# Loads of r, k and v from tile 9 on: issued by ScalarE instead of SyncE

## The chip, the cores and the metric

The kernel runs on one core of a Trainium2 chip. The core has five engines that run beside each other, each with its own in-order stream of instructions: TensorE (PE in the profile, its weight loads PEld), VectorE (DVE), ScalarE (ACT), GpSimd (POOL) and SyncE (SP). Transfers are done by 16 DMA engines; an instruction on SP or on ACT starts one. The metric is the time of one execution in microseconds of device time, smaller is better. The median of three runs before the change is 156.64 us (156.24 to 156.75).

## The reference

Two stages follow each other. The first is a linear attention with a decaying state, for batch 4, 8 heads, 768 time steps and head width 48:

```
for t in range(S):
    cur   = einsum('bhd,bhe->bhde', u * k[t], v[t])
    y[t]  = einsum('bhd,bhde->bhe', r[t], state + cur)
    state = w * state + einsum('bhd,bhe->bhde', k[t], v[t])
```

Its output, with the heads side by side, is x of shape (4, 768, 384). The second stage is a feed-forward block with a normalisation ahead of it and a residual:

```
xn  = (x - mean(x)) / sqrt(var(x) + 1e-6) * g_ln
out = x + relu(xn @ w_ch1) @ w_ch2        # 384 -> 1536 -> 384
```

All inputs and the output are 32-bit floats in the chip's main memory (HBM).

## The kernel before, in words

The 768 steps are cut into 6 chunks of 128, and a chunk of one batch entry is a tile: 24 tiles, numbered so that the four batch entries of a chunk follow each other. Every tile goes through the same steps. Each step is a small Python function with a two- or three-letter name, called with a tile's (or a block's) number and a letter for the engine: `v` is DVE, `s` is ACT, `g` is POOL, and `-` is a step whose engine is fixed.

For tile i the steps are these. LR, LK and LV load r, k and v (192 KB each, in runs of 48 floats; lines 326, 323 and 329). SR and SK multiply r and k by powers of the decay (line 194), CV turns v to bf16 (189 on ACT, 191 on POOL or DVE). TKR transposes both scaled tensors by DMA (line 490; tiles from 8 on; the earlier tiles are transposed on PE). AT multiplies them into the attention matrix (364), AM masks it, Q and S make the term with u and the state, CC copies a small result, VB and X put x together (427, 452). SQ and XN do the statistics and the centring (459; 465 on ACT, 467 elsewhere), LT2 (two tiles at once, line 484) or LTD (one tile, 480) transposes the centred tile by DMA. UP multiplies by the first weight (520) and RL is its relu (536 on ACT, 538 on DVE), DN multiplies by the second weight (548), OT adds the residual (604) and STO stores the tile (611, on SP or on ACT by its letter).

The feed-forward block works on groups of one or two tiles. UP writes into two PSUM buffers in turn, so the UP after the next one needs the RL of this one to be done. The loaded r, k and v have rings of 11 buffers each, the transposed tiles of 3, the centred tiles of 4.

The order of all this is one list, PLAN, written out in the source. A loop at the end of the kernel calls the steps in that order. Each engine carries out its own steps in the order of the list; waits between engines are added from the data and the buffers. So a step that is late holds up the steps that stand behind it in the list on the same engine, also when they need nothing of it. Every DMA also takes one of eight completion counters in turn, and waits until the DMA that held this counter before has landed.

In the kernel before, SP issues every load of r, k and v, the weights' loads, all DMA transposes and 16 of the 23 whole-tile stores. ACT issues a few loads of constants at the start and seven of the whole-tile stores. The functions that the change touches, and what calls them:

Of the kernel before, what the change touches and what calls it, by code (L numbers as in the profile page):

```python
# [22 lines left out]
S,1,- TCr,2,s XN,0,v SW,2,v SW,0,s DU,5,- AT,2,- LR,4,- CC,1,v Q,2,v Y,1,- AMb,2,v LT,0,- CV,2,s VB,1,g SQ,0,s XT,0,v
SW,1,g X,1,v ZU,1,v SR,3,g XN,1,s DU,26,- UP,0,- AMa,2,v LT,1,- S,2,- RL,0,s SW,5,g XT,1,v ZU,2,v SW,3,s DU,5,- TR,3,-
Y,2,- LK,4,- RS,0,g CC,2,v SW,4,v TCr,3,s VB,2,v DU,4,- UP,1,- X,2,v SW,7,s LW2,0,- SW,6,g UP,17,- TCk,3,v LV,4,- RL,1,s
XN,2,v AT,3,- SW,8,s Q,3,v LW2,1,- UP,16,- CV,3,v RL,17,s LW2,2,- S,3,- SR,4,g RL,16,v DU,2,- UP,2,- LK,5,- AM,3,v CC,3,s
SQ,1,s SK,4,g LT,2,- UP,18,- XT,2,s RL,2,s ZU,3,v RS,1,g TR,4,- LR,5,- RL,18,s VB,3,v UP,34,- CW,1,s TC,4,v CW,0,g Y,3,-
UP,32,- X,3,v CV,4,s AT,4,- Q,4,v RL,32,s DN,4,- AM,4,v XN,3,g RL,34,s S,4,- LR,6,- SQ,2,s LT,3,- UP,33,- CC,4,v XT,3,v
CW,3,s VB,4,v Y,4,- RL,33,v UP,49,- CW,2,s X,4,v UP,50,- CW,4,s LK,6,- XN,4,v DN,5,- CW,5,v RL,49,s LR,7,- LT,4,- SK,5,v
RL,50,s DN,6,- XT,4,v SR,5,v UP,48,- LV,5,- OT,1,v TR,5,- SK,6,v ZU,4,v LK,7,- SR,6,g DN,0,- TC,5,s DN,1,- LV,6,- AT,5,-  # L30
Q,5,g TR,6,- LV,7,- AM,5,v UP,64,- DN,2,- TC,6,s LR,8,- CV,5,g SR,7,v RL,48,s AT,6,- S,5,- LR,9,- OT,0,v SQ,4,s SK,7,g
Y,5,- CC,5,s RL,64,s DN,8,- LK,8,- AM,6,v VB,5,g TR,7,- RS,2,g LK,9,- UP,65,- UP,66,- Q,6,v TC,7,s X,5,v ZU,5,v DN,9,-
CV,7,g LV,8,- RL,66,s CV,6,g AT,7,- SQ,3,s RS,4,g XN,5,v LV,9,- Q,7,v S,6,- SR,8,v LT,5,- LR,10,- DN,10,- ZU,6,v SK,8,g
CC,6,s SQ,5,s RL,65,s XT,5,v Y,6,- STO,0,s AM,7,v S,7,- UP,81,- VB,6,g TKR,8,- LK,10,- SK,9,g OT,2,v UP,80,- CC,7,v X,6,v
SR,9,g DN,16,- RL,80,v XN,6,s Y,7,- CV,8,s RS,5,g DN,17,- VB,7,v TKR,9,- RL,81,s STO,1,- X,7,v CV,9,g DN,18,- ZU,7,v SQ,7,s
XN,7,g UP,82,- OT,4,v Q,8,g LT2,6,- AT,8,- RL,82,s DN,20,- LK,11,- AM,8,v LR,11,- SK,10,g S,8,- DN,21,- CC,8,s RS,3,g Y,8,-
SR,10,v AT,9,- LV,10,- TKR,10,- DN,22,- VB,8,g UP,97,- OT,5,v Q,9,g LR,12,- UP,100,- ZU,8,v RL,97,s X,8,v DN,12,- SK,11,g SQ,6,s
AM,9,v LK,12,- S,9,- RL,100,s SR,11,g XN,8,s UP,99,- DN,13,- STO,2,- CC,9,s RL,99,s RS,6,g VB,9,v TKR,11,- Y,9,- ZD,8,v LV,11,-
AT,10,- UP,96,- ZU,9,v Q,10,g X,9,v DN,14,- RL,96,v UP,98,- XN,9,g OT,3,v CV,10,s LT2,8,- UP,101,- RL,98,s AM,10,v SK,12,g STO,3,-
DN,28,- LR,13,- S,10,- Q,11,v DN,29,- RL,101,v CC,10,s VB,10,g CV,11,s AT,11,- ZU,10,v LK,13,- LV,12,- Y,10,- SR,12,g AM,11,v DN,30,-  # L40
UP,115,- TKR,12,- X,10,v S,11,- LR,15,- RL,115,s UP,116,- CC,11,v OT,7,v XN,10,s VB,11,g LK,14,- Y,11,- RL,116,v DN,24,- SR,13,g X,11,v
CV,12,s SQ,8,s UP,112,- UP,117,- SQ,9,s XN,11,g RL,117,v ZD,9,g LT2,10,- DN,25,- RL,112,v LR,14,- AT,12,- SK,13,g LV,13,- DN,26,- UP,113,-
Q,12,v TKR,13,- ZU,11,v SK,14,g UP,114,- RL,113,s LK,15,- STO,4,- OT,6,v S,12,- RL,114,s UP,132,- CC,12,v SQ,11,s VB,12,g DN,32,- LV,14,-
RL,132,s RS,7,g SR,14,v UP,128,- UP,133,- SQ,10,s AM,12,v LV,15,- ZD,11,g DN,33,- RL,128,s LK,16,- Q,13,v AT,13,- STO,5,s ZD,10,v DN,34,-
RL,133,s SK,15,g ZU,12,v Y,12,- CV,13,s TKR,14,- UP,129,- OT,8,v SR,15,g X,12,v S,13,- LR,16,- DN,36,- CC,13,v CV,14,s AM,13,v ZU,13,v
UP,131,- TKR,15,- XN,12,s RL,131,s RL,129,s SQ,12,s DN,37,- STO,6,- VB,13,g ZD,12,g Y,13,- RS,8,g DN,38,- CV,15,v X,13,v UP,130,- OT,9,v
XN,13,s AT,14,- Q,14,v RL,130,s DN,40,- LT2,12,- AM,14,v SQ,13,s SR,16,g LV,16,- S,14,- DN,41,- LK,17,- CC,14,s STO,7,s ZU,14,v RS,9,g
Y,14,- SK,16,v AT,15,- Q,15,v DN,42,- TKR,16,- AM,15,v ZD,14,g VB,14,g S,15,- LR,17,- UP,149,- CC,15,s ZD,13,g OT,10,v UP,145,- RL,149,s
LR,18,- X,14,v VB,15,g DN,44,- RL,145,v XN,14,s UP,148,- ZU,15,v CV,16,s LV,17,- Y,15,- SQ,14,s DN,45,- SK,17,v RL,148,s LK,18,- X,15,v
AT,16,- ZD,15,g DN,46,- SQ,15,s UP,144,- Q,16,v XN,15,s OT,11,v SR,17,g UP,147,- RL,144,s LT2,14,- AM,16,v S,16,- UP,146,- TKR,17,- CV,17,g  # L50
STO,9,- RL,147,v DN,52,- RL,146,s LK,19,- SK,18,v Y,16,- CC,16,s LR,19,- ZU,16,v DN,53,- SR,18,v UP,161,- ZD,16,v DN,54,- VB,16,v RL,161,s
STO,8,- Q,17,v UP,164,- X,16,v LV,18,- TKR,18,- UP,162,- OT,13,v RL,164,s LK,20,- SK,19,g AT,17,- UP,160,- AM,17,v SR,19,g S,17,- RL,160,s
DN,48,- ZU,17,v RL,162,s Y,17,- TKR,19,- XN,16,v CC,17,s DN,49,- VB,17,v LV,19,- UP,163,- X,17,v DN,50,- XN,17,v RL,163,s Q,18,v LT2,16,-
AT,18,- CV,18,s OT,12,v UP,165,- SK,20,g LR,20,- AM,18,v DN,56,- STO,10,- RL,165,s RS,10,g LK,21,- S,18,- Q,19,v DN,57,- CC,18,s SQ,16,s
ZU,18,v VB,18,g LR,21,- AT,19,- Y,18,- CV,19,g DN,58,- X,18,v LV,20,- ZD,17,g S,19,- AM,19,v UP,177,- SR,20,g UP,176,- STO,11,- RL,177,s
OT,14,v Y,19,- CC,19,s TKR,20,- RL,176,s DN,60,- LK,22,- SQ,17,s SK,21,v VB,19,v UP,179,- SR,21,g DN,61,- RL,179,v CV,20,g UP,180,- TKR,21,-
X,19,v XN,18,g DN,62,- ZU,19,v XN,19,s RS,11,g UP,178,- SQ,18,s LT2,18,- OT,15,v Q,20,g AT,20,- STO,13,- RL,180,s RL,178,v DN,68,- LR,22,-
AM,20,v UP,181,- STO,15,- ZD,18,g DN,69,- RL,181,s Q,21,v Y,20,- SQ,19,s LR,23,- LK,23,- SK,22,g DN,70,- AT,21,- LV,21,- OT,17,v S,21,-
UP,194,- CC,21,s ZD,19,v S,20,- UP,197,- AM,21,v SR,22,g CC,20,s STO,12,- RL,194,s DN,64,- VB,20,g RL,197,v TKR,22,- UP,192,- DN,65,- X,20,v
RL,192,s SR,23,g UP,193,- XN,20,s RS,12,g CV,21,s SK,23,v DN,66,- LTD,20,- RL,193,v LV,22,- UP,196,- VB,21,g OT,16,v STO,17,- Y,21,- RL,196,s  # L60
TKR,23,- Q,22,g UP,195,- X,21,v STO,14,- AT,22,- RL,195,s DN,76,- XN,21,g AM,22,v UP,208,- LTD,21,- SQ,21,s CV,22,s LV,23,- S,22,- DN,77,-
CC,22,v VB,22,v RL,208,s Y,22,- DN,78,- X,22,v UP,210,- OT,19,v XN,22,g AT,23,- Q,23,g SQ,20,s SQ,22,s RL,210,s LTD,22,- DN,72,- AM,23,v
UP,225,- RS,13,g CV,23,v DN,73,- RL,225,s UP,209,- RS,15,g STO,16,s DN,74,- RL,209,v RS,14,g S,23,- UP,242,- OT,18,v CC,23,s VB,23,g DN,80,-
RL,242,s STO,19,- Y,23,- DN,81,- X,23,v UP,224,- SQ,23,s DN,82,- RL,224,v XN,23,s RS,16,g UP,241,- OT,20,v LTD,23,- STO,18,s UP,226,- RL,241,s
DN,84,- RL,226,v UP,240,- DN,85,- RL,240,s STO,20,s DN,86,- UP,257,- OT,21,v UP,256,- STO,21,s RL,257,v DN,88,- RL,256,s DN,89,- DN,90,- OT,22,v
UP,258,- DB,0,- STO,22,- DA,0,- RL,258,s DB,1,- DA,1,- DB,2,- DA,2,- OB,23,v OA,23,v SB,23,s SA,23,-
"""


# [1 line left out]
def kernel(  # L71
# [23 lines left out]
    FK = F // P  # L95
# [27 lines left out]
    kf = ring("kf", [P, H, D], FP32)  # L123
    rf = ring("rf", [P, H, D], FP32)
    vf = ring("vf", [P, H, D], FP32)
# [70 lines left out]
    def issuer(e):  # L196
        return nc.scalar if e == "s" else nc.sync

    def chunk_src(t, i):
        c, b = divmod(i, B)  # L200
        return t[b, :, c * L : (c + 1) * L, :].rearrange("h t d -> t h d")
# [118 lines left out]
        copy(e, w2_sb[n][:, a * h : (a + 1) * h, :], w2_f(n)[:, a * h : (a + 1) * h, :])  # L320

    def LK(i, e):
        nc.sync.dma_start(out=kf(i)[:], in_=chunk_src(k, i))  # L323

    def LR(i, e):
        nc.sync.dma_start(out=rf(i)[:], in_=chunk_src(r, i))  # L326

    def LV(i, e):
        nc.sync.dma_start(out=vf(i)[:], in_=chunk_src(v, i))  # L329

    def SK(i, e):
        times(e, sck(i)[:, :, :D], kf(i)[:], Fk[:])
# [276 lines left out]
    def STO(i, e):  # L609
# [5 lines left out]
        UW=UW, WL=WL, LW1=LW1, SW=SW, LW2=LW2, CW=CW, LK=LK, LR=LR, LV=LV, SK=SK, SR=SR, CV=CV, TR=TR, TCr=TCr,  # L615
# [36 lines left out]
```

## Time and profile before

| | before |
|---|---|
| median of 3 runs | 156.64 us (156.24 to 156.75) |
| span of the profiled execution | 156.2 us |
| PE busy | 139.4 us (89%) |
| PEld busy | 106.5 us (68%) |
| DVE busy | 112.9 us (72%) |
| POOL busy | 87.9 us (56%) |
| ACT busy | 75.1 us (48%) |
| HBM read and written | 19.08 MB and 4.72 MB |
| granted TensorE clock | 1.000 |

The span runs from the first to the last instruction of the profiled execution; the median of the runs is 0.4 us above it. In the profile, a name with a `q` behind the engine (SPq, ACTq) is the engine's sequencer: there it issues DMAs or waits, and the engine is not counted as busy. In a timeline a row has the start in us, the duration in us, engine, line, operation, what is written and read, and how many instructions were merged; square brackets give the idle time before the row and what ended it. In a list of waits a row has who waited, for whom, the total in us, how often, and the longest.

### The profile page before, as it was taken

The numbers are of one execution on the slowest core, as the hardware profiler recorded it, in microseconds if no ns is written. First come the engines' busy times: TensorE is split into PE (matmuls) and PEld (weight loads), VectorE is DVE, ScalarE is ACT, GpSimd is POOL, SyncE is SP. The second block draws the span as 40 slices with busy tenths as digits, with TensorE's granted clock in tenths as the row PEclk, the third lists the DMA queues.
The fourth block names the chain that finished last, engine by engine and source line by source line (L and its number), as shares of the span: only waits on it lengthen the run. The fifth ranks groups of instructions, "written<-read, shape, count | busy, mean of one in ns | idle before, by whom it ended". The sixth has DMA issues, their size and how long they took to land.

```text
span 156.2 us, 4227 instructions
## 1 busy us (share of the span) xinstructions
PE 139.4 (89%) x1676; PEld 106.5 (68%) x1676; DVE 112.9 (72%) x224; ACT 75.1 (48%) x167; POOL 87.9 (56%) x127
## 2 busy tenths in 40 slices
PE   5659998999999869969969989998997999979991
PEld 1146687886778558757947767786775777758881
DVE  2149899996989856957659998899786767644421
ACT  3424666993766317135736547344253446615130
POOL 3016596503889979639739885134929885651000
PEclk9999999999999999999999999999999999999999
DMA  4999999988999979989989999999999898831221
GB/s 86 201 211 274 265 310 254 408 171 164 203 191 189 235 142 241 162 186 234 176 196 228 225 175 203 176 215 175 213 217 183 200 221 181 186 110 54 76 84 67
DMA packets 104465, 30.03 MB, mean 192 GB/s; under 512 B 99579, under 2 KB 102910, under 8 KB 104446
## 3 DMA queue, kind: packets, MB, share of 16 engines
q1 hardware_dynamic: 103132, 28.09, 89.4%
q10 hardware_dynamic: 1314, 1.67, 3.4%
q8 instruction: 13, 0.21, 0.6%
q14 instruction: 6, 0.05, 0.1%
HBM read 19.08 MB, written 4.72 MB: 152 GB/s over the span
## 4 chain that ended last, share of the span: by engine, by line
PE 29%; DMA 26%; SPq 21%; DVE 9%; POOL 5%; issue 4%; ACT 4%; ACTq 1%; DVEq 0%; POOLq 0%
PE hp L520 10%; PE o L548 9%; DMA xT<-xn 8%; DMA rf<-in_r_dram 8%; SPq L326 7%; SPq L329 5%; SPq L323 4%; DMA out_dram<-ot 3%; DMA w_all<-in_w_dram 2%; DMA kf<-in_k_dram 2%; DVE A L374 2%; POOL sc L194 2%; PE at L364 2%; PE o L261 2%; PE y L445 1%
## 5 line engine op out<-in xcount | busy, mean ns | idle before, releaser
L520 PE MATMUL hp<-xT,w_sb 128*128 128x128 bf16 (+1 forms) x612 | 57.1, 241 | 3.5 <-DMA xT<-xn 3.4
L548 PE MATMUL o<-w_sb,hT 128*128 128x384 bf16 x276 | 55.4, 326 | 0.6 <-DVE ot L604 0.4
L520 PEld LDWEIGHTS <-w_sb 128*128 128x128 bf16 x612 | 48.7, 114 | 8.4 <-DMA xT<-xn 3.2
L536 ACT ACTIVATE hT<-hp 128x512 bf16<-128x512 f32 x54 | 31.6, 595 | 34.4 <-PE hp L520 34.2
L548 PEld LDWEIGHTS <-hT 128*128 128x128 bf16 x276 | 24.2, 97 | 12.0 <-issue 0.8
L374 DVE TENSOR_TENSOR A<-at,mask 128x1024 bf16<-128x1024 f32 (+1 forms) x27 | 29.5, 1099 | 2.4 <-PE at L364 2.3
L194 POOL TENSOR_TENSOR sc<-kf,Fk 128x384 bf16<-128x384 f32 x15 | 15.4, 1026 | 14.9 <-DMA kf<-in_k_dram 9.0
L194 POOL TENSOR_TENSOR sc<-rf,Fr 128x384 bf16<-128x384 f32 x15 | 15.5, 1035 | 12.2 <-DMA rf<-in_r_dram 12.2
L604 DVE SCALAR_TENSOR_TENSOR ot<-o,rs,x 128x384 f32<-128x384 f32 x23 | 14.1, 614 | 8.7 <-PE o L548 4.3
L452 DVE SCALAR_TENSOR_TENSOR x<-y,Vb 128x384 f32<-128x384 f32 x24 | 13.2, 551 | 4.2 <-PE y L445 2.8
L427 POOL TENSOR_TENSOR Vb<-vf,cc 128x384 f32<-128x384 f32 x15 | 12.8, 850 | 6.0 <-DVE cc L191 4.3
L459 ACT ACTIVATE sqj<-x,sm 128x384 bf16<-128x384 f32 x24 | 14.7, 613 | 1.9 <-DVE x L452 1.8
L538 DVE TENSOR_SCALAR hT<-hp 128x512 bf16<-128x512 f32 x18 | 12.3, 686 | 3.1 <-PE hp L520 2.8
L364 PE MATMUL at<-trs 48*128 48x128 bf16 x192 | 10.0, 226 | 3.0 <-DMA trs<-sc 2.5
L476 POOL TENSOR_TENSOR rs<-rs,expo 128x1 f32<-128x1 f32 (+1 forms) x17 | 11.0, 649 | 1.4
L364 PEld LDWEIGHTS <-trs 48*128 48x128 bf16 x192 | 5.6, 97 | 8.6 <-DMA trs<-sc 3.9
L261 PE MATMUL o<-warm 128*128 128x512 bf16 x23 | 9.4, 533 | 2.0 <-DVE warm L226 2.0
L189 ACT CAST vv<-vf 128x384 bf16<-128x384 f32 x13 | 6.6, 509 | 9.2 <-DMA vf<-in_v_dram 7.8
L194 DVE TENSOR_TENSOR q<-trs 128x512 bf16<-128x512 bf16 x16 | 8.9, 555 | 2.6 <-DMA trs<-sc 2.5
L189 ACT COPY trs<-tr 128x512 bf16<-128x512 bf16 (+1 forms) x8 | 5.9, 747 | 9.3 <-PE tr L345 7.6
L194 POOL TENSOR_TENSOR q<-trs 128x512 bf16<-128x512 bf16 x8 | 9.6, 1196 | 0.9 <-PE hp L520 0.8
L445 PE MATMUL y<-vv,A 128*128 128x48 bf16 x192 | 8.8, 185 | 0.6 <-ACT vv L189 0.4
(76 smaller groups left out, 168.2 us busy)
## 6 DMA issues: line engine op xcount, KB each, us to landing
rf<-in_r_dram SPq DMA_DIRECT2D x24, 192.0 KB, 3.6
kf<-in_k_dram SPq DMA_DIRECT2D x24, 192.0 KB, 4.0
vf<-in_v_dram SPq DMA_DIRECT2D x24, 192.0 KB, 4.3
w_f<-in_moe_w_ch_dram SPq DMA_DIRECT2D x6, 768.0 KB, 6.1
out_dram<-ot SPq DMA_DIRECT2D x16, 192.0 KB, 3.6
out_dram<-ot ACTq DMA_DIRECT2D x7, 192.0 KB, 3.6
trs<-sc SPq DMA_TRANSPOSE x16, 3.5
w_all<-in_w_dram ACTq DMA_DIRECT2D x1, 192.0 KB, 3.8
```

The source lines that it names most:

```text
L189: nc.scalar.copy(out=out, in_=in_)
L194: engines[e].tensor_tensor(out=out, in0=in0, in1=in1, op=ALU.mult)
L261: nc.tensor.matmul(out=warm_ps[0][:], lhsT=warm[:], rhs=warm[:].unsqueeze(1).to_broadcast([P, 4, P]), start=True, stop=True)
L364: nc.tensor.matmul(out=t[:, par, q, :], lhsT=trs(i)[p0 : p0 + D, 1, q, :], rhs=trs(i)[p0 : p0 + D, 0, q, :], start=True, stop=True,)
L374: nc.vector.tensor_tensor(out=AA(i)[:, a:b].rearrange("p e q t -> p (e q) t"), in0=psum["at", i][:, a:b].rearrange("p e q t -> p (e q) t") ...
L427: engines[e].tensor_tensor(out=Vb(i)[:].rearrange("p (h d) -> p h d", h=H), in0=vf(i)[:], in1=cc(i)[:].unsqueeze(2).to_broadcast([P, H, D] ...
L452: nc.vector.scalar_tensor_tensor(out=xx(i)[:], in0=psum["y", i][:, :C], scalar=1.0, in1=Vb(i)[:], op0=ALU.mult, op1=ALU.add, accum_out=sm[ ...
L459: nc.scalar.activation(out=sqj[:], in_=xx(i)[:], func=ACT.Square, bias=sm[i][:], scale=-float(C), accum_out=sq[g][:, j : j + 1])
L520: nc.tensor.matmul(out=t[:, a * gw : (a + 1) * gw].rearrange("p (j t) -> p j t", j=size), lhsT=w1_sb[n][kc][:, fb::FB], rhs=xT(g)[:, :size ...
L536: nc.scalar.activation(out=o, in_=s, func=ACT.Relu)
L548: nc.tensor.matmul(out=psum["o", i][:, :C], lhsT=hT(g)[:, fk, j * P : (j + 1) * P], rhs=w2_sb[d][:, a, :], start=(fk == 0), stop=(fk == FK ...
L604: nc.vector.scalar_tensor_tensor(out=ot(i), in0=psum["o", i][:, :C], scalar=rs[g][:, j : j + 1], in1=xx(i)[:], op0=ALU.mult, op1=ALU.add,)
```

## The change

All loads of r, k and v from tile 9 on (15 tiles, 45 loads) get the letter `s` in PLAN, and the three load functions issue from the engine of the letter. The place of each load in the list stays, and so do all other steps; PLAN is only wrapped into lines anew, five fewer than before, so that lines behind it have numbers smaller by five. On PE, DVE and POOL the instructions and their order are the same. SP goes from 125 instructions to 80, and the 45 loads stand between the activations, copies and stores of ACT. The loads of tiles 0 to 8, the weights, the transposes and SP's stores stay on SP.

```diff
-TC,6,s LR,8,- CV,5,g SR,7,v RL,48,s AT,6,- S,5,- LR,9,- OT,0,v SQ,4,s SK,7,g
+TC,6,s LR,8,- CV,5,g SR,7,v RL,48,s AT,6,- S,5,- LR,9,s OT,0,v SQ,4,s SK,7,g
...
-Q,12,v TKR,13,- ZU,11,v SK,14,g UP,114,- RL,113,s LK,15,- STO,4,- OT,6,v
+Q,12,v TKR,13,- ZU,11,v SK,14,g UP,114,- RL,113,s LK,15,s STO,4,- OT,6,v
...
     def LK(i, e):
-        nc.sync.dma_start(out=kf(i)[:], in_=chunk_src(k, i))
+        issuer(e).dma_start(out=kf(i)[:], in_=chunk_src(k, i))
 
     def LR(i, e):
-        nc.sync.dma_start(out=rf(i)[:], in_=chunk_src(r, i))
+        issuer(e).dma_start(out=rf(i)[:], in_=chunk_src(r, i))
 
     def LV(i, e):
-        nc.sync.dma_start(out=vf(i)[:], in_=chunk_src(v, i))
+        issuer(e).dma_start(out=vf(i)[:], in_=chunk_src(v, i))
```

`issuer(e)` was there before: it is `nc.scalar` for the letter `s` and `nc.sync` otherwise.

More of the change, by code (lines that the diff above doesn't have):

```diff
@@ L23 @@
[L23 to L49, printed above, removed]
@@ L67 @@
+UP,209,- RS,15,g STO,16,s DN,74,- RL,209,v RS,14,g S,23,- UP,242,- OT,18,v CC,23,s VB,23,g DN,80,- RL,242,s STO,19,- Y,23,- DN,81,- X,23,v UP,224,-
+SQ,23,s DN,82,- RL,224,v XN,23,s RS,16,g UP,241,- OT,20,v LTD,23,- STO,18,s UP,226,- RL,241,s DN,84,- RL,226,v UP,240,- DN,85,- RL,240,s STO,20,s
+DN,86,- UP,257,- OT,21,v UP,256,- STO,21,s RL,257,v DN,88,- RL,256,s DN,89,- DN,90,- OT,22,v UP,258,- DB,0,- STO,22,- DA,0,- RL,258,s DB,1,- DA,1,-
+DB,2,- DA,2,- OB,23,v OA,23,v SB,23,s SA,23,-
 """
```

60 lines of the change are left out of this document (39 added, 21 removed).

## The prediction

> **What bounds the kernel now.** I read the page's busy slices and chain first, then the busy times of the stretch that the change touches, then who waits for whom, then the timeline of SP beside that of ACT in one stretch.
>
> ```profile
> DMA  4999999988999979989989999999999898831221
> ```
>
> ```profile
> PE 29%; DMA 26%; SPq 21%; DVE 9%; POOL 5%; issue 4%; ACT 4%; ACTq 1%; DVEq 0%; POOLq 0%
> ```
>
> ```profile
> 40.00:136.00 96.00, 89.38 (x1068) 68.69 (x1066) 76.82 (x142) 47.11 (x113) 66.63 (x88) 1.00 1.08 198
> ```
>
> The row of the stretch from 40 to 136 us has the length, then the busy time of PE, PEld, DVE, ACT and POOL, the granted clock, the share of the DMA engines and GB/s. The first 40 us stay as they are, since the first moved load is issued at 40.61 us. From 40 to 136 us PE is busy for 89.38 of 96 us, so whatever the change removes is at most the 6.6 us between, and a little of the end. But PE is not alone: the DMA engines show nine tenths nearly everywhere, and a fifth of the chain is SP's sequencer, which only issues transfers. What PE waits for by name:
>
> ```profile
> PE hp L520 <- DMA xT<-xn: 3.4, 3, 1.2
> PE at L364 <- DMA trs<-sc: 2.5, 3, 1.2
> ...
> PE s L395 <- DVE q L194: 0.5, 1, 0.5
> PE o L548 <- DVE ot L604: 0.4, 1, 0.4
> PE y L445 <- ACT vv L189: 0.4, 1, 0.4
> ```
>
> Four of the five end in transfers: the two kinds of transposes, q (made from the transposed tile), and vv (made from the loaded v). Upstream, the makers of the transposes' inputs wait for the loads:
>
> ```profile
> POOL sc L194 <- DMA kf<-in_k_dram: 9.0, 4, 5.2
> ACT vv L189 <- DMA vf<-in_v_dram: 7.8, 4, 3.5
> ```
>
> These are sums from 40 to 136 us: 17 us of waits in two groups alone, for loads that come just in time. Why they come so late shows in SP's timeline:
>
> ```profile
> 76.76 0.57 SPq L323 DMA_DIRECT2D kf<-in_k_dram  x1
> 77.38 1.84 SPq L611 DMA_DIRECT2D out_dram<-ot  x1
> 79.26 1.21 SPq L329 DMA_DIRECT2D vf<-in_v_dram  x2
> 80.51 1.40 SPq L323 DMA_DIRECT2D kf<-in_k_dram  x1
> 82.08 1.53 SPq L490 DMA_TRANSPOSE trs<-sc  x1
> ```
>
> Each row begins where the one before ended, up to 0.17 us: SP's queue is full, and a load stands behind transposes that wait for POOL, and behind stores that nobody needs soon.
>
> **The change part by part.** *Off SP.* 45 loads go, 15 of each kind:
>
> ```profile
> L326 SPq DMA_DIRECT2D rf<-in_r_dram x24: 425/582/4276, 0.7 to 122.5; - x24
> ...
> DMA to landing us min/median/max: 2.8/3.6/6.1
> ```
>
> ```profile
> L323 SPq DMA_DIRECT2D kf<-in_k_dram x24: 433/704/3085, 3.7 to 122.9; - x24
> ```
>
> ```profile
> L329 SPq DMA_DIRECT2D vf<-in_v_dram x24: 433/715/2272, 4.5 to 134.0; - x24
> ```
>
> By the medians that is 15 x (0.58 + 0.70 + 0.72) = 30 us of SP's 96 us. What stays there (transposes and stores) is issued as soon as its input stands.
>
> *Onto ACT.* The same 30 us go to ACT's sequencer. ACT is busy for 47 of the 96 us, so 77 of 96 would be taken. Most of it need not even stand beside idle time, by these rows of ACT:
>
> ```profile
> 75.11 1.25 ACT L536 ACTIVATE hT<-hp 128x512 bf16<-128x512 f32 x2 [1.57 <-PE hp L520]
> 76.26 0.61 ACT L459 ACTIVATE sqj<-x,sm 128x384 bf16<-128x384 f32 x1
> ...
> 76.86 0.59 ACT L536 ACTIVATE hT<-hp 128x512 bf16<-128x512 f32 x1
> 77.34 0.62 ACT L459 ACTIVATE sqj<-x,sm 128x384 bf16<-128x384 f32 x1
> ...
> 78.00 0.60 ACT L536 ACTIVATE hT<-hp 128x512 bf16<-128x512 f32 x1
> 78.01 0.35 ACTq L611 DMA_DIRECT2D out_dram<-ot  x1
> ```
>
> The store at 78.01 starts 0.01 us after the relu before it starts, and runs beside it for 0.35 of the relu's 0.60 us. So I let a load on ACT start when the ACT instruction before it in PLAN starts. An issue up to about 0.6 us then costs the next activation nothing; a longer one costs the excess, where the next activation is not waiting anyway.
>
> *When the loads start.* In this stretch, by PLAN: K of tile 15 stands behind the relu of 75.11, against 76.76 on SP; V of 14 behind 76.26, against 79.26; V of 15 behind 77.34, against about 79.8 (second of the pair); K of 16 behind 78.00, against 80.51. Four loads start 1.6 to 3.0 us sooner. The first and the last of the 45:
>
> ```profile
> 40.61 0.70 SPq L326 DMA_DIRECT2D rf<-in_r_dram  x1
> 134.00 0.58 SPq L329 DMA_DIRECT2D vf<-in_v_dram  x1
> ```
>
> ```profile
> 40.39 0.60 ACT L536 ACTIVATE hT<-hp 128x512 bf16<-128x512 f32 x1
> 132.22 0.51 ACT L189 CAST vv<-vf 128x384 bf16<-128x384 f32 x1 [0.88 <-DMA vf<-in_v_dram]
> ```
>
> R of tile 9 stands behind a relu that starts at 40.39, a lead of 0.2 us; V of 23 behind a CAST at 132.22, a lead of 1.8 us. Laid out so, 43 of the 45 lead, typically by 1 to 3 us. Two are later, because ACT itself waits for a load ahead of them, K of 13 and V of 12 behind it:
>
> ```profile
> 65.79 1.62 SPq L323 DMA_DIRECT2D kf<-in_k_dram  x1
> ```
>
> ```profile
> 67.88 0.51 ACT L189 CAST vv<-vf 128x384 bf16<-128x384 f32 x1 [2.32 <-DMA vf<-in_v_dram]
> ```
>
> That CAST waits for a v that should lead by about 2 us itself, so they come out about even. I take 1.5 us as the typical lead.
>
> *Waits that are added.* A moved load also waits for one of the eight completion counters, whose last holder may now be a transpose on SP. Behind such a wait stand ACT's relus, and behind them PE. A counter comes round after eight DMAs, some 7 us at the pace of SP's rows above; loads land a median 3.6 us after issue, 6.1 at most. I cost it at nothing; without this cover one such wait would cost about a microsecond of ACT.
>
> *What PE gets.* The transposes of sc (16, line 490) start sooner twice: their inputs by up to the loads' lead, and their issue by SP's emptier queue. The three waits of 2.5 us are none longer than 1.2 us, so a lead of 1.5 us closes them, and q's 0.5 and vv's 0.4 with them: 3.4 us. The xT transposes hang on XN, which hangs on PE's own order, not directly on the loads; I leave their 3.4 us standing; the far end of the gain has one of these three waits, 1.1 us, closed as well.
>
> *What is late next.* The loads, started sooner, meet the transposes in the same 16 engines, whose share is already 1.08. The xT transposes are issued by rows like this:
>
> ```profile
> L484 SPq DMA_TRANSPOSE xT<-xn x7: 1211/1271/1726, 52.6 to 119.3; - x7
> ```
>
> Between nothing and a new wait on each of the seven here, I take one more of the existing size, 1.1 us, since three xT transposes wait today and the seven and their neighbours are as tightly placed. And ACT's bursts (three loads in a row at 68 us and at 122 us, 2.1 us by the medians) can hold a relu that PE needs: between nothing and 0.7 us each, I take 0.3 us in all.
>
> **Sum.** -3.4 + 1.1 + 0.3 = -2.0 us against the span of 156.2, so a span of 154.2; the median of the runs is 0.4 us above the span, so 154.6 us.
>
> **The rivals.** *Nothing moves, because the DMA engines are the bound.* If a share of 1.08 means that no load can land sooner from whichever queue, the leads become queueing, PE's waits stay, and the time is 156.6 us. For it speaks the row of nines. Against it: loads of r land a median 3.6 us after issue and the fastest in 2.8, so the engines do not queue much. The Trainium skill, DMA: Bandwidth & Descriptors, section "Issuing engines are not separate DMA queues", says that DMAs from several engines end on the same 16 engines, and that a second issuer only saves issue time, usually little. By that rule the time is this rival's; but the trace shows a fifth of the chain in SP's issuing, which the rule takes to be small.
>
> *Slower: the relus stand behind the issues.* A transpose takes 1.21 us to issue at least. If a load on ACT takes 1.2 us, because both sequencers share what makes the descriptors or the ring fills, ACT needs 47 + 54 of 96 us. The place is relu to UP. After the relu of 76.86 PE leaves 0.35 us:
>
> ```profile
> 77.14 1.47 PE L520 MATMUL hp<-xT,w_sb 128*128 128x256 bf16 x12
> ```
>
> Its first half runs to about 77.8, and the second needs that relu, done at 77.45. With 1.2 us an issue, the loads of 75.11 and 76.26 hold the relu back by 1.0 us, which makes PE 0.65 us late. Laid out over the 45 loads, relus at four places hold PE by 2.9 us in all, and the loads lose their lead: 159.5 us. At 0.8 us an issue the same laying-out holds PE by nothing; it decides from about 1.1 us. Against it: the median issue of 0.6 to 0.7, and the store of 78.01, which took 0.35 us while SP's store beside it took 1.84. No row shows an issue on ACT beside a transpose. The Trainium skill, Perfetto Trace Analysis, "DMA Instruction — HWDGE (DVE, Sync)", describes one descriptor generator that two sequencers share, locked by the one that uses it; by this the rival is likelier than the rows alone make it.
>
> *Slower: the transposes lose their place in the DMA engines.* On one queue a transpose has ahead of it what SP issued before. With loads on a second queue, later loads can share the engines with it. One load's data beside each transpose is about 1 us more to landing (192 KB at the 198 GB/s of the stretch's row). The three xT waits grow by 1.0 each, and a fourth appears here, where the chain that ended last runs through a transpose though PE shows no gap:
>
> ```profile
> 96.27 3.69 DMA xT<-xn
> ```
>
> That is +4.0, and of the 3.4 us gained on the sc transposes 2.8 remain: 157.8 us. It decides from about 0.7 us a transpose.
>
> **How the numbers follow.** Forecast 0.50, DMA-bound 0.12, transposes late 0.20, relus late 0.18. The measurement tells about 0.3%, 0.5 us, from no change. Faster is the forecast's 0.50, the DMA-bound case gives 0.10 for within and 0.02 for slower, and the other two make slower 0.40. The forecast's own range is 152.1 (all 3.4 and the 1.1, nothing lost) to 156.1. Taken to the other side up to 159.0, which keeps most of the relus' case, the range is 152.1 to 159.0.
>
> **What would show it.** SP's timeline from 46 us on has idle gaps, and the chain's SPq share falls well below 21%. ACTq rows for the loads last 0.4 to 0.7 us and start with the activation before them. The waits of POOL for kf and rf fall to less than half, the waits of PE for trs go, those for xT stay. It is wrong if issues on ACT last over 1 us, if PE waits for hT or hp's buffers through ACT L536's successor, or if the xT transposes wait more often than three times.

## The result: slower by 1.4%

The changed kernel takes 159.04 us (median of 20 runs, 156.62 to 160.59) against 155.91 us for the kernel before in the same comparison (153.92 to 157.40). The ratio is 1.0139, 95% interval 1.0106 to 1.0172: some 2.2 us slower. Here and below a ratio compares fast runs alone, leaving out those over 1.5% above the fastest run of their kernel (11 of the 20 of the changed kernel), while a median is of all runs, so the quotient of the two medians above is larger, 1.020. The prediction was 2.0 us faster.

The granted clock of the kernel before, in 40 slices of the span:

```profile
PEclk9999999999999999999999999999999999999999
```

The page of the changed kernel, first the busy slices, then the queues and the chain:

```profile
PEclk9955699999999995999999999999999999999999
DMA  4999999988999999279999699599999997641221
...
q1 hardware_dynamic: 56332, 19.24, 54.3%
q10 hardware_dynamic: 48114, 10.53, 34.1%
...
PE 52%; DMA 19%; DVE 14%; POOL 5%; issue 3%; ACTq 2%; ACT 2%; DVEq 0%; POOLq 0%
```

SP's sequencer, 21% of the chain before, is gone from it. q10 holds what ACT issues, the loads above all. New is the 5 in the middle of PEclk. The 5s near the start are not: most profiles of the runs below have them, whichever queue the loads are on, and the last section says why the first row shows none.

SP's timeline in the changed kernel now has holes, as between the third and the fourth of these rows:

```profile
50.69 1.23 SPq L485 DMA_TRANSPOSE trs<-sc  x1
51.96 0.58 SPq L606 DMA_DIRECT2D out_dram<-ot  x1
52.94 1.21 SPq L479 DMA_TRANSPOSE xT<-xn  x1
55.60 1.23 SPq L485 DMA_TRANSPOSE trs<-sc  x1
```

The makers of the transposes' inputs hardly wait for loads any more. Before, POOL waited 9.0 us for kf from 40 to 136 us, and for rf as in the first of the next rows; the last two rows are of the changed kernel, where POOL no longer waits for kf:

```profile
POOL sc L194 <- DMA rf<-in_r_dram: 5.1, 5, 3.0
```

```profile
POOL sc L189 <- DMA rf<-in_r_dram: 2.2, 3, 1.0
...
POOL vv L186 <- DMA vf<-in_v_dram: 0.5, 1, 0.5
```

An issue on ACT begins with the activation ahead of it and runs beside it:

```profile
75.31 0.62 ACT L454 ACTIVATE sqj<-x,sm 128x384 bf16<-128x384 f32 x1
75.31 0.37 ACTq L321 DMA_DIRECT2D rf<-in_r_dram  x1
```

So what the change was to do upstream it did. PE's waits from 40 to 136 us are these:

```profile
PE hp L515 <- DMA xT<-xn: 4.1, 3, 2.5
PE hp L515 <- DVE hT L533: 0.8, 1, 0.8
PE hp L515 <- ACT hT L531: 0.7, 1, 0.7
PE s L390 <- DVE q L189: 0.4, 1, 0.4
PE at L359 <- DMA trs<-sc: 0.2, 1, 0.2
```

The waits for trs went from 2.5 to 0.2 us. Those for xT went from 2.4 us in two to 4.1 us in three, one of which is now 2.5 us long:

```profile
PE hp L520 <- DMA xT<-xn: 2.4, 2, 1.2
```

This row is of the kernel before, from 40 to 136 us. The 3.4 us in three waits that the prediction shows are of its whole run, with one wait at 139 us; over the whole run the step is from 3.4 to 4.1 us. Two waits are new: UP waits for a relu.

The clearest view takes PE from its first matmul of S 5, just ahead of the first moved load, to its last matmul: 1250 matmuls in every kernel that has none added. The columns are the window, its length, PE's busy time and number of matmuls, PEld, DVE, ACT and POOL, the granted clock, the DMA share and GB/s. First the kernel before, then the changed one:

```profile
41.02:153.07 112.05, 104.37 (x1250) 81.16 (x1246) 82.17 (x153) 51.06 (x121) 69.59 (x93) 1.00 0.96 181
```

```profile
41.88:155.68 113.80, 107.42 (x1250) 82.91 (x1246) 80.96 (x153) 51.06 (x121) 68.83 (x92) 0.94 0.89 176
```

Length less busy time is what PE stands idle: 7.7 us before, 6.4 after. In this execution PE waits 1.3 us less and yet takes 1.75 us more, because the same 1250 matmuls take 3.05 us more at a clock of 0.94. Part of that is this execution's own: its clock is granted at 0.95 for long stretches, which no other profile here shows, and at 160.59 us it is the longest of the 20 runs. How far the two kernels differ in PE's busy time is therefore better read from a pair further down (the buffers of hp). But the 0.50 in the middle comes back in many of the kernels below. It stands right behind the wait of 2.5 us:

```profile
59.25 2.44 PE L515 MATMUL hp<-xT,w_sb 128*128 128x256 bf16 x12 [2.51 <-DMA xT<-xn]
```

```profile
59.50:62.90 3.40, 3.40 (x20) 2.18 (x18) 0.03 (x1) 2.29 (x5) 1.82 (x4) 0.50 1.10 251
```

The first row is PE's timeline, the second the windows view of the same kernel. Twelve matmuls take 2.44 us where twelve of the same kind took 1.47 us in the kernel before.

### The profile page after: what moved, and what is told of

Same layout as the page of the kernel before. It is cut to its first block, busy times and chain, and to the rows that moved or that the text cites. A ratio compares the mean times of both kernels' runs of the same rounds, so it can differ in the third digit from the quotient of the medians.

```text
span 158.8 us, 4227 instructions
## 1 busy us (share of the span) xinstructions
PE 142.4 (90%) x1676; PEld 108.3 (68%) x1676; DVE 112.7 (71%) x224; ACT 75.0 (47%) x167; POOL 87.7 (55%) x127
## 4 chain that ended last, share of the span: by engine, by line
PE 52%; DMA 19%; DVE 14%; POOL 5%; issue 3%; ACTq 2%; ACT 2%; DVEq 0%; POOLq 0%
PE o L543 19%; PE hp L515 19%; DMA xT<-xn 10%; DMA trs<-sc 3%; PE at L359 3%; DVE A L369 3%; DMA w_all<-in_w_dram 2%; DMA rf<-in_r_dram 2%; PE tr L340 2%; PE y L440 2%; DVE Vb L422 2%; PE o L256 2%; POOL Vb L422 2%; DMA rows<-in_moe_g_ln_dram 2%; DVE x L447 1%
## 5 line engine op out<-in xcount | busy, mean ns | idle before, releaser
L515 PE MATMUL hp<-xT,w_sb 128*128 128x128 bf16 (+1 forms) x612 | 59.2, 246 | 5.6 <-DMA xT<-xn 4.1
L515 PEld LDWEIGHTS <-w_sb 128*128 128x128 bf16 x612 | 49.9, 114 | 11.3 <-issue 5.3
L543 PE MATMUL o<-w_sb,hT 128*128 128x384 bf16 x276 | 57.5, 336 | 0.0
L599 DVE SCALAR_TENSOR_TENSOR ot<-o,rs,x 128x384 f32<-128x384 f32 x23 | 14.1, 614 | 10.3 <-PE o L543 6.3
L256 PE MATMUL o<-warm 128*128 128x512 bf16 x23 | 8.9, 507 | 1.9 <-DVE warm L221 1.9
L189 DVE TENSOR_TENSOR q<-trs 128x512 bf16<-128x512 bf16 x16 | 9.5, 597 | 0.0
L189 DVE TENSOR_TENSOR sc<-rf,Fr 128x384 bf16<-128x384 f32 x9 | 6.5, 723 | 4.2 <-DMA rf<-in_r_dram 4.2
L189 POOL TENSOR_TENSOR Z<-ZS,WLZ 128x384 bf16<-128x384 f32 x8 | 8.4, 1055 | 1.7 <-DVE ZS L416 1.6
```

The source lines that it names most:

```text
L189: engines[e].tensor_tensor(out=out, in0=in0, in1=in1, op=ALU.mult)
L256: nc.tensor.matmul(out=warm_ps[0][:], lhsT=warm[:], rhs=warm[:].unsqueeze(1).to_broadcast([P, 4, P]), start=True, stop=True)
L515: nc.tensor.matmul(out=t[:, a * gw : (a + 1) * gw].rearrange("p (j t) -> p j t", j=size), lhsT=w1_sb[n][kc][:, fb::FB], rhs=xT(g)[:, :size ...
L543: nc.tensor.matmul(out=psum["o", i][:, :C], lhsT=hT(g)[:, fk, j * P : (j + 1) * P], rhs=w2_sb[d][:, a, :], start=(fk == 0), stop=(fk == FK ...
L599: nc.vector.scalar_tensor_tensor(out=ot(i), in0=psum["o", i][:, :C], scalar=rs[g][:, j : j + 1], in1=xx(i)[:], op0=ALU.mult, op1=ALU.add,)
```

## The experiments

Three theories went into the first runs. A: loads on a second queue share the DMA engines with the transposes, which land later (the prediction's third rival). B: what ACT does for others stands behind the added issues (the second rival). C: loads tied to ACT's progress start too late whenever ACT is late. D and E came from the traces. Every ratio is to the kernel before, with its 95% interval. In the diffs `-` and `s` are a step's letters in PLAN.

**ACT's time alone.** The loads stay on SP; in each moved load's place ACT gets a copy of about 0.4 us.

```diff
-LR,9,s
+LR,9,- AD,0,s
...
+    def AD(i, e):
+        nc.scalar.copy(out=dum[1][:], in_=dum[0][:])
```

> Loads stay on SP as before; at each of the 45 places where the change puts a load, ACT gets a copy of 128x230 floats instead (about 0.4 us, as long as an issue on ACT took in the changed kernel). It measures ACT's added work alone. Theory A (with the loads on a second queue, transposes and loads share the DMA engines and the transposes land later): no change, within 0.5 us of before. Theory B (ACT's own items stand behind the added issues): slower by most of the 2.2 us that the change cost (1.4%), 1.5 to 2.5 us. Theory C (loads tied to ACT's progress start too late after any delay): no change.

Measured: 157.77 us, ratio 1.0052 (1.0009 to 1.0095). ACT's busy time in the window from S 5 on grew from 51.06 to 63.86 us. Work of the issues' size on ACT costs something, but little over a third of the loss, and an issue runs beside an activation while these copies do not. B called for 1.5 to 2.5 us and 0.8 came, so B alone does not explain the loss.

**Half of the tiles each.** Only tiles 16 to 23, then only tiles 9 to 15 have their loads on ACT.

```diff
-LK,16,- ... LV,23,-
+LK,16,s ... LV,23,s
```

> Only the 24 loads of tiles 16 to 23 are issued by ACT. In the traces the changed kernel loses about 4.5 us of position on ACT between 45 and 104 us and wins some 2 us of it back afterwards. Theory A: the loss belongs to the transposes of the tiles up to 15; this half is no slower than before, 0 to 1.5 us faster. Theory B: the cost goes with the number of loads, 24 of 45, 1.2 us slower. Theory C: the same as A in sign, about 0 to 1 us faster.

> Only the 21 loads of tiles 9 to 15 are issued by ACT. Theory A: nearly the whole loss is here, 2 to 3.5 us slower than before. Theory B: 21 of 45 of it, 1.0 us slower. Theory C: 2 to 3.5 us slower, with late landings of k, r and v rather than of the transposes.

Measured: tiles 16 to 23 take 156.39 us, ratio 0.9937 (0.9905 to 0.9968); tiles 9 to 15 take 159.44 us, ratio 1.014 (1.0096 to 1.0185). In this pair the whole loss lies with tiles 9 to 15. There PE's busy time is that of the kernel before and its idle time is 8.9 us, without any drop of the clock:

```profile
41.04:154.23 113.19, 104.31 (x1250) 81.25 (x1246) 84.48 (x153) 50.89 (x121) 69.94 (x93) 1.00 0.91 180
```

**Stores in place of loads.** Loads on SP, the 16 whole-tile stores of SP on ACT.

```diff
-STO,1,-
+STO,1,s
```

> All loads stay on SP as before; the 16 whole-tile stores of SP go to ACT, so that SP is relieved of 16 issues (about 9 us) that nobody waits for, and the second queue carries stores only. Theory A (a second queue hurts by its share of the engines): stores are 128 packets a tile against the loads' 1024, so little harm, and SP's loads and transposes start sooner: 0.5 to 1.5 us faster. Theory B: 16 more issues on ACT, 0.3 to 0.8 us slower. Theory C: faster by 0.5 to 1.5 us.

Measured: 159.33 us, ratio 1.0107 (1.0059 to 1.0155). Other transfers of 192 KB on the second queue cost about as much. That goes against C, which is about the loads' starts, and against A as it stood: both called for 0.5 to 1.5 us less, and B for only 0.3 to 0.8 us more. The profiled execution is the shortest of the twelve (156.90 us) and has no drop of the clock behind S 5, so it does not show where the time went; this loss stays unexplained.

**The buffers of hp (theory D).** The text ahead of the prediction says that UP takes two PSUM buffers in turn. That is not always so: which of the two is taken is the framework's choice. In the changed kernel's instruction stream, UP 101 waits for ACT (the relu of UP 98, just ahead of it) where it waited for DVE (the relu of UP 96), and UP 146 likewise got the buffer just ahead. PE's timeline, changed kernel first:

```profile
66.59 0.84 PE L515 MATMUL hp<-xT,w_sb 128*128 128x256 bf16 x6
68.11 0.84 PE L515 MATMUL hp<-xT,w_sb 128*128 128x256 bf16 x6 [0.69 <-ACT hT L531]
```

```profile
62.91 1.47 PE L520 MATMUL hp<-xT,w_sb 128*128 128x256 bf16 x12
```

In the kernel before the two blocks are one row, back to back. Two kernels force the turn, the changed one and, as a control, the one before:

```diff
-    ps_h = ctx.enter_context(tc.tile_pool(name="ps_h", bufs=2, space=bass.MemoryType.PSUM))
+    ps_h = [ctx.enter_context(tc.tile_pool(name=f"ps_h{a}", bufs=1, space=bass.MemoryType.PSUM)) for a in range(2)]
...
+    next_hp = lambda: ps_h.append(ps_h.pop(0)) or ps_h[1].tile([P, 512], FP32, name="hp")
...
-        t = psum["hp", g, m] = ps_h.tile([P, 512], FP32, name="hp")
+        t = psum["hp", g, m] = next_hp()
...
```

> The changed kernel with the two PSUM buffers of hp taken strictly in turn, so that UP 101 and UP 146 wait for the relu of the UP two places back, as in the kernel before; in the changed kernel the framework had put them into the buffer of the UP just ahead. Theory D (the buffer choice, an unmeant part of the change, is most of the loss): PE's gaps of 0.68 us at UP 101 and 0.82 us at UP 146 go, and with what they delayed the kernel comes within 0.5% of the kernel before, about 157.0 us. Theory A (transposes land later with loads on a second queue): the gaps at UP 97 (2.5 us), UP 132 and UP 149 stay, the time is still over 1% above the kernel before, about 158.2 us. Theory C (loads tied to ACT's progress): the same as A.

> Control: the kernel before with the two buffers of hp taken strictly in turn. Its waits at UP 101 and UP 146 are those of the kernel before; those at UP 81, 80 and 82 differ. All theories: within 0.4% of the kernel before, 156.1 to 157.3 us, with no gap of PE over 0.4 us at UP 80 to 82. If it is faster by more, the buffer choice costs the kernel before something as well.

Measured: the changed kernel 159.87 us, ratio 1.0218 (1.017 to 1.0267); the control 156.77 us, ratio 1.0019 (0.9983 to 1.0054). The two waits of 0.7 and 0.8 us are gone from the trace, and the kernel is no faster. D falls. These two are the cleanest pair, since the control has the same buffers. Their windows, control first:

```profile
41.23:152.44 111.21, 104.48 (x1250) 81.26 (x1246) 83.74 (x152) 51.02 (x121) 70.12 (x93) 1.00 0.93 183
```

```profile
41.41:154.76 113.35, 105.76 (x1250) 82.04 (x1246) 83.94 (x152) 51.00 (x121) 69.80 (x93) 0.98 0.92 179
```

2.14 us longer: 1.28 of it busy time at a lower clock, 0.86 idle time (7.59 against 6.73).

**Less data in the loads.** From tile 11 on only two of eight heads are loaded (48 KB a load), by SP and by ACT; the other heads keep an older tile's data.

```diff
-        issuer(e).dma_start(out=kf(i)[:], in_=chunk_src(k, i))
+        issuer(e).dma_start(out=kf(i)[:, :NHL(i), :], in_=chunk_src(k, i)[:, :NHL(i), :])
```

> The kernel before with loads of two heads out of eight for each tile from 11 on (48 KB in place of 192), all issued by SP; the other six heads hold an older tile's data. The reference for the next run. All theories: faster than the kernel before, by up to the transposes' waits, 153.5 to 155.5 us; the xT waits fall by half if the loads' data is what holds the transposes up.

> The changed kernel with the same small loads (two heads of eight from tile 11 on), issued by ACT from tile 9 on; the hp buffers fall out as in the kernel before here. Theory A (loads' data beside the transposes): with a quarter of the data the loss is gone, at most 0.3% above the same loads on SP, and SP's freed time shows as a gain, 152.5 to 155 us. Theory B (ACT's own items behind the issues): it stays 0.8 to 1.4% above the same loads on SP. Theory C (late starts): 0.3 to 1% above, with waits of POOL for kf and rf after each delay of ACT. Theory D: within 0.4% of the same loads on SP or faster, since the buffers are right.

Measured: on SP 153.54 us, ratio 0.9747 (0.9698 to 0.9797); on ACT 154.66 us, ratio 0.9891 (0.9852 to 0.9929). The ratios are 1.4% apart, as much as the loss with whole loads, where A called for at most 0.3%; B's 0.8 to 1.4% fits them. The traces show no difference: from S 5 to the last matmul the two take 108.39 and 108.36 us. But the six runs on SP fall into three of 151.5 to 152.7 and three of 154.4 to 154.6 us; the profile is of the second kind, and the ratio rests on the first. What sets the two kinds apart was not caught in a trace, so this pair speaks against A and settles nothing.

**By place.** With the buffers in turn, eight loads that ACT issues while an xT transpose is under way go back to SP; and the reverse, these eight alone on ACT.

```diff
-LK,11,s LR,11,s LV,10,s LR,12,s LR,14,s LV,13,s LV,16,s LK,17,s
+LK,11,- LR,11,- LV,10,- LR,12,- LR,14,- LV,13,- LV,16,- LK,17,-
```

> The changed kernel with the hp buffers in turn, but eight loads go back to SP: those that ACT issues while an xT transpose is under way (K 11, R 11, V 10 and R 12 behind LT2 6; R 14 and V 13 behind LT2 10; V 16 and K 17 behind LT2 12). 37 loads stay on ACT. Theory A (loads on the second queue share the DMA engines with a transpose and make it late): most of the loss goes, LT2 6 lands within 4.8 us of its issue (6.0 with all on ACT, 4.2 with all on SP), LT2 10 and 12 within 3.2 us, and the time is at most 0.6% above the kernel before, 155.5 to 157.7 us. Theories B and C (issues on ACT, or starts tied to ACT, whichever load it is): 37 of 45 loads still cost their share, 1.3 to 2% above, 158.8 to 159.9 us.

> The complement: only these eight loads are issued by ACT, the other 37 by SP, hp buffers in turn. Theory A: eight loads carry most of the loss, 0.8 to 1.8% above the kernel before, 158.0 to 159.5 us, with LT2 6 at 5.5 us or more and LT2 10 and 12 at 4 us or more from issue to landing. Theories B and C: a fifth of the loss, at most 0.4% above, up to 157.4 us.

Measured: 37 loads on ACT 162.97 us, ratio 1.0145 (1.006 to 1.0231); the eight alone 161.73 us, ratio 1.0144 (1.0061 to 1.0227). B and C fall with the second: eight loads should have cost a fifth. A's sum falls with the first, which was to come within 0.6%. The waits show more, first with the eight on SP, then with the eight on ACT (both profiled executions are the longest of their six, so the sizes are large ones):

```profile
PE at L359 <- DMA trs<-sc: 7.7, 5, 3.1
```

```profile
PE hp L515 <- DMA xT<-xn: 6.1, 4, 2.3
```

With the eight on SP, PE waits 0.5 us for xT in all, as A says, and 7.7 us for trs: the lateness went to the other transposes. That the remaining 37 loads, which run beside these, are the reason was not tried by itself. In both kernels the idle time also drew the clock down (busy 107.96 and 107.87 us in place of 104.5):

```profile
40.85:159.58 118.73, 107.96 (x1250) 82.96 (x1246) 82.80 (x153) 50.58 (x121) 70.41 (x93) 0.96 0.88 172
```

```profile
42.35:158.84 116.49, 107.87 (x1250) 82.67 (x1246) 82.63 (x153) 51.08 (x121) 68.42 (x92) 0.97 0.87 171
```

The issue rows of single transposes (last number: us from issue to landing) make it plain. LT2 12, with V 16 and K 17 behind it, in the kernel before and with the eight on ACT:

```profile
xT<-xn SPq DMA_TRANSPOSE x1, 2.5
```

```profile
xT<-xn SPq DMA_TRANSPOSE x1, 6.7
```

The same rows for all (LT2 6 has loads of tiles 10 to 12 beside it; the last column is the median of the 16 transposes of sc):

| kernel | loads beside LT2 6 | LT2 6 | loads beside LT2 12 | LT2 12 | trs<-sc |
|---|---|---|---|---|---|
| before | SP | 4.6 | SP | 2.5 | 3.5 |
| before, buffers in turn | SP | 4.2 | SP | 2.5 | 3.5 |
| tiles 16 to 23 on ACT | SP | 4.1 | ACT | 5.1 | 3.9 |
| tiles 9 to 15 on ACT | ACT | 5.3 | SP | 2.5 | 3.6 |
| changed | ACT | 6.3 | ACT | 5.0 | 4.3 |
| changed, buffers in turn | ACT | 6.0 | ACT | 4.8 | 4.2 |
| the eight on SP | SP | 3.5 | SP | 2.5 | 4.8 |
| the eight on ACT | ACT | 5.2 | ACT | 6.7 | 3.7 |

The two halves cross over: the transpose that is late is the one that has loads of ACT beside it. LT2 10, which has R 14 and V 13 beside it, goes the same way: 2.5 to 3.5 us with these two on SP, 4.3 to 5.2 us on ACT. The other kernels of this document bear LT2 12 out and even show a dose. In all nine with both of its loads on SP it takes 2.5 to 2.7 us; with one on ACT, in the two runs by kind at the end, 3.9 and 3.8 us; with both, 4.8 to 6.7 us; with both at a quarter of the size, 3.3 us. LT2 6 is less clean: in one of the kernels with added matmuls it took 4.7 us with its loads on ACT, hardly more than the 4.6 us of the kernel before. So that loads on the second queue make a transpose land late is shown, and this part of A stands. It does not hold for all of them: the median of all eleven xT transposes fell, from 3.1 us before to 2.5 us in the changed kernel.

**Tiles 16 to 23 with the buffers in turn.**

> Loads of tiles 16 to 23 alone on ACT (24 loads), with the hp buffers in turn, so that UP 146 no longer waits for the relu just ahead (0.85 us in the run of the same loads with the framework's choice, which took 0.9937 of the kernel before). Theory D in its small form (a wrong buffer costs its own gap and no more): 0.988 to 0.992, about 155.2 us. If the buffers do not matter: 0.994 again, 155.8 us.

Measured: 158.05 us, ratio 1.0063 (1.0025 to 1.0101), slower than without the turn. The trace has two waits that the first run of these loads did not have, 1.9 us at UP 149 (LT2 12 took 6.0 us) and 1.6 us ahead of DN 48, each with a drop of the clock behind it. The two traces are the extremes, though: this execution is the longest of its twelve (161.80 us), that of the first run the shortest (155.12 us).

**The clock (theory E).** E: a wait of PE much over 1.5 us is followed by 3.4 us of halved clock. Two kernels fill the wait at UP 97 with dummy matmuls, the changed one and the one with buffers in turn; one puts a long wait into the kernel before and leaves every load on SP.

```diff
+        for _ in range({97: 6}.get(i, 0)):
+            nc.tensor.matmul(
+                out=t[:], lhsT=warm[:], rhs=warm[:].unsqueeze(1).to_broadcast([P, 4, P]), start=True, stop=True
+            )
```

```diff
-CC,8,s
+CC,8,s GT,8,s
...
+    def GT(i, e):
+        for _ in range(i):
+            nc.scalar.copy(out=gate[:], in_=gsrc[:])
...
+        if i == 97:
+            nc.tensor.matmul(out=t[:, :P], lhsT=gate[:, :P], rhs=warm[:], start=True, stop=True)
```

> The kernel before, with eight extra copies of 128x512 on ACT (in a stretch of 3.9 us in which ACT waits) and one small matmul at the head of UP 97 that reads the last copy, so that PE's wait of about 1.2 us there becomes one of 2.2 to 2.8 us. All loads stay on SP. Theory E: the clock record shows 0.5 for 3.4 us behind that gap, and the time grows by the gap's 1.0 to 1.6 us and 1.2 to 1.7 us more, together 2 to 3 us, 1.013 to 1.02. Theory A alone: the gap's own 1.0 to 1.6 us at most, 1.006 to 1.010, less what later waits take up.

> The changed kernel with six dummy matmuls of 512 columns (about 1.3 us) at the head of UP 97, written into UP 97's own buffer before its real matmuls, where PE stood idle for 2.5 us. (With them the framework gives UP 101 the buffer that it has in the kernel before.) Theory E (a long idle time of PE halves the clock for 3.4 us): no record of 0.5 near 60 us, the rest of the gap stays under 1.3 us, and the time falls by 1.2 to 2.2 us (clock, and 0.7 for the buffer), to about 157.3 us, 0.2 to 0.6% above the kernel before. Theory A alone (only the transposes' lateness counts): the gap is filled but ends when it ended, and the time falls by the buffer's 0.7 us at most, still over 0.9% above.

> The same six dummy matmuls in the changed kernel with the hp buffers in turn (which took 1.0218 of the kernel before, with one record of 0.5 for 3.4 us at 60 us), so that nothing but the dummies differs between the two. Theory E: 1.2 to 1.7 us less, 1.011 to 1.014. Theory A alone: 1.02 again, within 0.3%.

Measured: the wait put in gives 160.26 us, ratio 1.0195 (1.0136 to 1.0254). Its timeline at UP 97, and the windows behind it:

```profile
59.52 0.23 PE L521 MATMUL hp<-warm,gate 128*128 128x128 bf16 x1 [3.22 <-ACT gate L224]
59.59 2.20 PE L525 MATMUL hp<-xT,w_sb 128*128 128x256 bf16 x12
```

```profile
60.20:63.60 3.40, 3.40 (x22) 2.23 (x21) 0.00 (x0) 2.30 (x6) 2.12 (x4) 0.50 1.00 223
```

```profile
40.49:155.90 115.41, 106.23 (x1251) 81.86 (x1247) 83.24 (x153) 56.15 (x129) 69.69 (x93) 0.99 0.88 176
```

The wait became 3.2 us where it was 1.2, PE's busy time grew from 104.37 to 106.23 us, and the loads had no part in it. E's mechanism is shown, on a wait somewhat longer than aimed at.

The fills: 160.87 us, ratio 1.0127 (1.002 to 1.0234), for the changed kernel; 160.05 us, 1.0207 (1.0132 to 1.0283), with buffers in turn. In both traces the drop at 60 us is gone, as E says, and from S 5 to the last matmul the second takes 112.01 us, 1.34 less than without the fill:

```profile
42.01:154.02 112.01, 105.52 (x1256) 81.83 (x1252) 84.19 (x153) 50.89 (x121) 70.05 (x92) 1.00 0.92 179
```

But the timed runs give no sign of it: both ratios are close to those without the fill (1.0139 and 1.0218), where E called for 0.2 to 0.6% and 1.1 to 1.4% over the kernel before, though the intervals are wide enough to touch these. So it is not shown that the drop at this one place carries the loss. That other waits, which differ from one execution to the next, take its place is possible, and not shown either.

**A better version?** Tiles 16 to 23 on ACT once more, and the same without V 16 and K 17.

> Loads of tiles 16 to 23 alone on ACT, once more, as the candidate for a better version: 0.9937 of the kernel before in its first comparison. If that stands, 0.991 to 0.997; a ratio above 0.998 says that the first was luck. Theory E: where single runs are slow, they are those with a clock record of 0.5 in the middle.

> Loads of tiles 16 to 23 on ACT but for V 16 and K 17, which ACT issued while the transpose LT2 12 was under way (5.1 us from issue to landing in the run of all 24 such loads, 2.5 us in the kernel before). Theory A: LT2 12 lands in under 3.2 us, PE's wait at UP 149 goes, and the ratio is 0.989 to 0.995, better than both kernels. If the gain of the 24 loads was luck, or if two loads behind transposes on SP cost as much: 0.996 to 1.004.

Measured: 157.41 us, ratio 0.9979 (0.9931 to 1.0028), the second time; 157.56 us, 1.0031 (0.9987 to 1.0074), without the two loads. LT2 12 landed in 2.7 us, as A says, and the wait moved to the next transpose: PE waits 2.0 us at AT 16. The first 0.6% of gain did not come again clearly. No version here clearly beats the kernel before.

**By kind.** v alone, then k and r alone, from tile 9 on.

```diff
-LK,9,s LR,9,s LV,9,s
+LK,9,- LR,9,- LV,9,s
```

> Only the loads of v from tile 9 on are issued by ACT (15 of 45). Theory A, dose by number: a third of the loss, 1.003 to 1.008. Theory C: v is read on ACT, DVE and POOL some 10 us after its issue, later than k and r are needed, so no start is too late: within 0.3% of the kernel before, or faster by what SP gets free.

> Only the loads of k and r from tile 9 on are issued by ACT (30 of 45). Theory A, dose by number: two thirds of the loss or more, 1.008 to 1.016. Theory C: the whole loss, 1.012 to 1.018, with POOL's waits for kf and rf as in the changed kernel. Theory E on both: where the time is over 1.01, some runs show a clock record of 0.5 in the middle (a mean clock of 0.989, which none of 79 runs of the kernel before had).

Measured: v alone 157.49 us, ratio 1.0044 (1.0001 to 1.0087); k and r 161.49 us, 1.0199 (1.0099 to 1.0299). The first is a third of the loss, as A has it; the second is no less than the whole, above A's range of 0.8 to 1.6% and C's of 1.2 to 1.8%. The median of the trs transposes goes with it: 3.5 us before, 3.7 with v, 4.6 with k and r.

## Why the prediction was wrong

*Off SP* held. SP has holes, 17 of the 27 transposes are issued 0.03 us after their input stands (9 before), and SP's sequencer left the chain.

*Onto ACT* held. The median issue on ACT is 0.37 to 0.40 us for the three kinds (0.6 to 0.7 was assumed), and it begins with the activation ahead. The row of r has minimum, median and maximum in ns:

```profile
L321 ACTq DMA_DIRECT2D rf<-in_r_dram x15: 374/382/1410, 40.3 to 124.8; - x15
```

The longest took 1.7 us, and no activation that PE needed stood behind it. Twenty of the 45 run while SP issues a transpose, and their median is 0.39 us against 0.38 for the others, so the two issuers do not hold each other up. The rival of the late relus, which called for 1.1 us an issue, is out.

*When the loads start* held: POOL's waits for kf and rf fell from 14.1 to 2.2 us, to less than the half that was named. This is so in the profile of the changed kernel; with the buffers in turn POOL again waits 6.6 us for kf.

*Waits that are added* held for the completion counters: no wait for one is seen that cost PE anything. Two issues of 1.7 and 1.4 us at 54.6 and 56.4 us lie in a stretch in which ACT has nothing else to do, and what lengthened them is open (the DMA that held the second one's counter had landed by 52.4 us). Another kind of added wait was overlooked, the two UPs that wait for the relu just ahead, because the two hp buffers were taken to be used in turn; a wait of UP for the relu ahead was among the prediction's own signs of being wrong. It was 1.5 us in the trace, but taking it away gained nothing.

*What PE gets* held for trs and vv, and nearly for q: 3.4 us were to close, 2.8 did (2.5 + 0.5 + 0.4 against 0.2 + 0.4).

*What is late next* named the right place and had the wrong size. This is the first step that failed. For all that the moved loads do to the transposes one more xT wait of 1.1 us was taken; in the trace the xT waits up to 136 us grew by 1.7 us, those of the whole run by 0.7 us, with one wait of 2.5 us among them. What was missed is how late single transposes become: the three xT transposes that have loads beside them, LT2 6, 10 and 12, land 1.7, 1.5 and 2.5 us later, the trs transposes 0.8 us later in the median. That is the third rival's mechanism, "+1 us a transpose", whose 157.8 us, 1.2 above the median before, was about half of what was measured. The Trainium skill's rule that queues of several engines end on the same DMA engines (DMA: Bandwidth & Descriptors, "Issuing engines are not separate DMA queues") was weighed as a reason for no change. The traces agree that the engines are shared: LT2 12 takes 2.5 us with the same two loads behind it on SP's queue and about 5 us with them on ACT's. What it means here is worse than no gain, since order on one queue had also been priority.

The *sum* failed too, at a term that it did not have: PE's busy time was taken to stay. Idle time alone fell from 7.7 to 6.4 us in the profiled execution, 1.3 of the 2.0 us forecast, while the same matmuls took 3.05 us more, some of which is that execution's own. In the pair with the buffers in turn both go the wrong way: 0.86 us more idle time and 1.28 us more busy time. The prediction added up waits as if three of 1.2 us and one of 2.5 us plus small ones were alike. They are not: after the long one the clock was halved for 3.4 us, which costs some 1.3 to 1.9 us of PE (1.28 in the pair; 1.86 with the wait put in, of which the added matmul is 0.2). (In the windows from S 5 on, PE is busy for 103.7 to 104.5 us in all kernels without such a drop and without added matmuls, 105.8 to 106.2 with one, 107.5 to 108.0 with two; the changed kernel's own 107.42, with one drop and the 0.95 besides, stands apart.)

The *baseline* was off too: the median was taken to lie 0.4 us above the span of the profiled execution. The changed kernel's profiled execution has a span of 158.8 us and a time of 160.59 us. If the same 1.8 us lie around the span before, the execution that the prediction read was itself about 1.4 us slower than the median, and its waits may have been larger than usual.

What stays open is how the 2.2 us divide between longer waits and the lower clock. The changed kernel's trace has it all in the clock, the run of tiles 9 to 15 all in the waits (8.9 us idle, clock 1.00), and the pair with buffers in turn in both. Four of the 20 runs of the changed kernel have a mean clock of 0.989, which the profile with k and r on ACT has with one drop of 3.4 us, and three have 0.957 or less; none of 102 runs of the kernel before has such a mean. One of the 20 has 1.000. So the drop is in some of its runs, not in all. Open too is why the stores on ACT, which leave LT2 6 and LT2 12 at 3.4 and 2.7 us, cost nearly as much as the loads. That a second queue makes a transpose late, and that a long wait of PE halves the clock, is shown; that the two together are the whole loss is not.

## What to carry to other kernels

Before bulk loads go to a second queue, ask which short, urgent transfer stands ahead of them on the first: there its place in the queue is its priority, on two queues it shares the engines, and a full queue can be doing useful ordering. PE's waits should be read one by one and not only as a sum, since here every wait of 2.25 us or more was followed by a halved clock, and none up to 1.45 us was. And a change that leaves an engine's order untouched can still alter its waits through the buffers that the framework picks, so the waits in the two instruction streams are worth comparing.

## What the runs showed of the hardware

The granted clock falls after surprisingly short waits. Counting every profile from S 5 on, but for its last microseconds: waits of PE up to 1.45 us were never followed by a drop; of fifteen from 1.5 to 2.2 us five were (1.52, 1.77 and 1.92 among them) and ten were not (1.72, 1.96 and 2.12 among them); all five from 2.25 to 3.22 us were. Each drop reads 0.50 for 3.4 us, or for 6.8 us in the case of the wait of 3.14, which began within the wait. The Trainium skill (TensorE: Matmul & The Clock Gate, "HAM oscillation — how this bites in real kernels") puts the rule as no idle gap of PE over about 3.4 us. That limit does not agree: waits of less than half of that were enough in some cases here.

A mean clock of 1.000, as the kernel before has in the table ahead of the prediction, does not say that the head of the kernel ran at full clock. In that profile the record of the clock begins only at 18.0 us, and what has no record counts as full. Two warm-up matmuls at 16.5 us took 1.06 us there; in the changed kernel with the buffers in turn, whose record reads 1.00 from 15.7 us on, the same two took 0.59 us.

An issue on ACT took 0.37 to 0.40 us in the median, against 0.6 to 0.7 for the same loads on SP before, and it ran beside the activation.
